# The last 64 keys of a block-causal attention: high and low halves of the probabilities on 128 partitions

## The chip, the core and the metric

The kernel runs on one core of a Trainium2 chip. The metric is the device time of one execution in microseconds (us). PE is TensorE, with its weight loads as a row of their own (PEld); DVE is VectorE, ACT is ScalarE, POOL is GpSimd and SP is SyncE, which issues most DMA transfers here.

## The reference

Attention over 4 batches, 8 heads, 576 positions and head dimension 64, whose output goes through two expert layers. Positions are in nine blocks of 64; a query sees the keys of its own block and of all blocks before it.

```python
scores = scale * np.matmul(q, k.transpose(0, 1, 3, 2))
mask = block_i >= block_j                  # block = position // 64
attn = softmax(np.where(mask, scores, -1e9))
x = np.matmul(attn, v)                     # (4, 8, 576, 64) -> rows of 512
x = moe(x, ...)                            # top 2 of 8 experts, 512 -> 1024 -> 512
out = moe2(x, ...)                         # one of 8 experts, with a bias by modality
```

The change is in the attention alone.

## The kernel before, in words

Attention goes through 16 pairs of heads (`pair(p)`, line 849). Numbers are split into a high part, rounded to the type that TensorE takes in one pass, and a low part, the rest; a product is hi x hi + hi x lo + lo x hi or, for the values, two halves side by side.

For each pair:

- `TQ`, `TK` and `T4` transpose q and k on PE, 128 positions at a time; `T4` (line 896) does the last 64 positions of q and of k, each as a transpose of 64 partitions. ACT writes the high parts (`qh` with its blocks in tiles named `kp`, `kh`), DVE the low ones (`ql`, `kl`).
- `S0` to `S8` are the scores of the nine query blocks, both heads on the 128 partitions of one product: three matmuls each (`ps<-kh,kp`, `ps<-kl,kp`, `ps<-kh,kp`). `M` is the row maximum on DVE (`nm`), `E` the exponential on ACT, which writes the strips `p` and sums the rows into `ss`. `R` adds the two sums of the last block, `R1` adds 1e-9 to the nine sums (`ss`, 128x9), `R2` makes their reciprocals (four `RECIPROCAL rr<-ss`).
- `B0` to `B5` transpose the probabilities, 128 keys by 128 columns at a time (`pt<-ident,p`), up to four in one PSUM bank; ACT copies the high part into `PTh` (`H`), DVE the low part into `PTl` (`L`). Of query block 8 the last 64 keys are left over: `BT` (line 1015) transposes them to 64 partitions, `HT` and `LT` write them to slot 28 of `PTh` and `PTl`. Slots 25 to 27 are zero on those partitions.
- `VX` and `V0`, `V1` (`av(h)`, line 1036) multiply by the values, `pa<-PTh,vs` and `pa<-PTl,vs`. The high and the low 64 columns of v are the 128 columns of the weights, so a full sum comes out as two halves of 64 partitions that `X0`, `X1` add (`pt<-IW,oT`). `V0` and `V1` have five matmuls for `PTh` and five for `PTl`: 448, 448, 320 and 256 columns with 128 keys each, and 256 columns with the last 64 keys on 64 partitions.
- `CX`, `C0`, `C1` and `XC0`, `XC1` are ACT's copies from PSUM (`oT`, `xu`). POOL multiplies the result by the reciprocals (`x` and the small `LH`, line 1067). It also splits v into high and low parts, `VS` (line 860): a cast and a subtraction for 128 partitions, and both again for the last 64 keys on 64.

Loads go through SP's queue (`load`, line 830): q and k three pairs ahead, v two. Of each tensor's tile of 128x5x2x64 the fifth chunk holds the last 64 positions on 64 partitions.

What stands where on PE, ACT and DVE is set by a planner (lines 1201 to 1350): a table of due times and costs for each kind of instruction, from which it places one step after the other on the engine that is free first. Three PSUM buffers serve all transposes and `X` products (`ps_t`), in turn: a new one waits until the last reader of the third one before it is done. Into the same engines it puts the routing of the experts after pairs 7, 11 and 15, a serial chain that is mostly DVE's (`sl_ob`, `sl_oa` are its one-hot tables, `sl_ov` POOL's product of them). After attention the expert layers follow, laid out by the same clock of planned costs.

Of the kernel before, what the change touches and what calls it, by code (L numbers as in the profile page):

```python
# [7 lines left out]
F32 = mybir.dt.float32  # L8
F32R = mybir.dt.float32r
BF16 = mybir.dt.bfloat16  # L10
I32 = mybir.dt.int32
AF = mybir.ActivationFunctionType
# [18 lines left out]
def moe_kernel(tc, q, k, v, w_gate, w_noise, noise, w1, w2, mod_id, w_gate2, mod_bias, m2w1, m2w2, out):  # L31
    nc = tc.nc
    B, H, S, D = q.shape
# [67 lines left out]
    gps = Timed(nc.gpsimd, "pool", pool_cost)  # L101
    vec, ten, act = Timed(nc.vector, "dve", dve_cost), Timed(nc.tensor, "pe", pe_cost), Timed(nc.scalar, "act", act_cost)

    with ExitStack() as top:
# [12 lines left out]
        ident = cst.tile([128, 128], F32, name="ident")  # L117
# [667 lines left out]
        with ExitStack() as ph:  # L785
            ld = ph.enter_context(tc.tile_pool(name="ld", bufs=3))
            aw = ph.enter_context(tc.tile_pool(name="aw", bufs=1))
# [3 lines left out]
            ps_t = ph.enter_context(tc.tile_pool(name="ps_t", bufs=bk[1], space=PSUM))  # L791
            ps_a = ph.enter_context(tc.tile_pool(name="ps_a", bufs=bk[2], space=PSUM))

            PTh = aw.tile([128, 29, 2, 64], F32R, name="PTh")
            PTl = aw.tile([128, 29, 2, 64], F32R, name="PTl")
            QB = [[keep.tile([128, 1280], F32R, name="kp%d" % (i + 2 * j))[:, 0:NB * 128].rearrange("p (b h s) -> p b h s", b=NB, h=2)
                   for j in range(2)] for i in range(2)]
            PW = [128 * ((i + 2) // 2) for i in range(8)] + [576]
# [28 lines left out]
            def copy(o, i):  # L827
                act.activation(o, i, AF.Copy)

            def load(p, names):  # L830
                b, hp = divmod(p, HP)
                r = L.setdefault(p, {})
                src = {"q": q, "k": k, "v": v}

                def ends():
                    for n in names:
                        nc.sync.dma_start(r[n][0:64, 4, :, :], src[n][b, 2 * hp:2 * hp + 2, 512:576, :].rearrange("h p d -> p h d"))
                for n in names:
                    r[n] = ld.tile([128, 5, 2, D], F32, name=n + "ld", bufs=2 if n == "v" else 3)
                if p:  # L840
                    ends()
                for n in names:
                    for i in range(2):
                        nc.sync.dma_start(r[n][:, 0:4, i, :],
                                          src[n][b, 2 * hp + i, 0:512, :].rearrange("(c p) d -> p c d", p=128))
                if not p:
                    ends()

            def pair(p):

                b, hp = divmod(p, HP)
                r = L[p]
                st = {}
                P = PP[p % 2]
                qh, ql = QB[0][p % 2], QB[1][p % 2]
                rr, xu = RR[p % 3], XU[p % 2]
                f = {}


                def VS():  # L860
                    vs = st["v"] = aw.tile([128, 5, 2, 2, D], F32R, name="vs", bufs=2)
                    for pp, c0, c1 in ((128, 0, 4), (64, 4, 5)):
                        hi = vs[0:pp, c0:c1, :, 0, :]
                        src = r["v"][0:pp, c0:c1]
                        gps.tensor_copy(hi, src)
                        gps.tensor_sub(vs[0:pp, c0:c1, :, 1, :], src, hi.bitcast(F32))

                def tr(n):
                    pt = ps_t.tile([128, 4, 128], F32, name="pt")
# [25 lines left out]

                def T4():
                    pt = ps_t.tile([128, 2, 64], F32, name="pt")
                    for i, n in enumerate("qk"):
                        ten.transpose(pt[:, i, :], r[n][0:64, 4].rearrange("p h d -> p (h d)"), ident[0:64, 0:64])
                    st["t4"] = pt  # L900

                def A4():
# [110 lines left out]
                    bank(m)  # L1013

                def BT():
                    st["bt"] = ps_t.tile([64, 128], F32, name="pt")
                    ten.transpose(st["bt"], P[8][:, 512:576], ident)

                end = lambda T: T[0:64, 28].rearrange("p h s -> p (h s)")
                f.update(BT=BT, HT=lambda: act.activation(end(PTh), st["bt"], AF.Copy),  # L1020
                         LT=lambda: vec.tensor_sub(end(PTl), st["bt"], end(PTh).bitcast(F32)))


                w = lambda j, h, n=128: st["v"][0:n, j, h].rearrange("p a d -> p (a d)")

                def VX():
                    pX = st["ax"] = ps_a.tile([128, 2, 256], F32, name="pa")
# [8 lines left out]
                def av(h):  # L1036
                    def V_():
                        pa = st["a", h] = ps_a.tile([128, 448], F32, name="pa")
                        for i, T in enumerate((PTh, PTl)):
                            ten.matmul(pa, w(0, h), T[:, 2:9, h, :], start=(i == 0), stop=False)  # L1040
                            ten.matmul(pa, w(1, h), T[:, 9:16, h, :], start=False, stop=False)
                            ten.matmul(pa[:, 128:448], w(2, h), T[:, 16:21, h, :], start=False, stop=False)
                            ten.matmul(pa[:, 192:448], w(3, h), T[:, 21:25, h, :], start=False, stop=False)
                            ten.matmul(pa[:, 192:448], w(4, h, 64), T[0:64, 25:29, h, :], start=False, stop=(i == 1))
                    f["V%d" % h] = V_
                    f["C%d" % h] = lambda: copy(st["oT"][:, h, 128:576], st["a", h])

# [44 lines left out]
            pads(0)  # L1092
            nc.gpsimd.memset(PTh[:, 21].bitcast(F32), 0.0)
            nc.gpsimd.memset(PTl[:, 21].bitcast(F32), 0.0)
            nc.gpsimd.memset(PTh[0:64, 25:28].bitcast(F32), 0.0)
            nc.gpsimd.memset(PTl[0:64, 25:28].bitcast(F32), 0.0)
            zeros(1, gps)
            pads(1)

# [206 lines left out]
            while any(todo.values()) or len(aside) > 1 or "early" not in flags:  # L1306
                best = None
                for e, l in todo.items():
                    c = []
                    for i, (due, p, n) in enumerate(l[:60]):  # L1310
                        t = earliest(e, p, n)
                        if t is not None:
                            c.append((t, due, i))
                    if c:
                        m = min(c)[0]
                        t, _, i = min((x for x in c if x[0] <= m + eps), key=lambda x: x[1])
# [6 lines left out]
                if aside:  # L1323
                    t = max(aside[0][0], clk["dve"])
                    if best is None or t <= best[0] and (t <= dve_next or t > aside[0][0] + patience):
                        best = (t, None, 0)
                t, e, i = best
# [3 lines left out]
                if e:  # L1331
                    _, p, n = todo[e].pop(i)
# [6 lines left out]
                else:  # L1339
                    clk["base"] = t  # L1340
                    d = next(aside[0][1], None)
# [204 lines left out]
        with tc.For_i(0, nc.values_load(more[0:1, 0:1], min_val=0, max_val=1), 1), tc.tile_pool(name="r1", bufs=1) as r1:  # L1546
# [12 lines left out]
            with tc.For_i(0, nc.values_load(eo[0:1, NG2:], min_val=0, max_val=NG2), 1):  # L1559
                NT2 = G2 // 128  # L1560
                a, bl = done(row_col(r1, ovs.rearrange("p c k -> p (c k)"), 2 * nb))
                pl = ps_r.tile([128, NV, NT2], F32, name="pt")
                for i in range(B):
                    n = slice(10 * i, 10 * i + 10)
# [12 lines left out]
                for t in range(NT2):  # L1577
                    xr = rp.tile([128, DM], F32, name="xr", bufs=5)
                    gps.indirect_dma_start(out=xr, out_offset=None, in_=X1, in_offset=bass.IndirectOffsetOnAxis(ap=ido[:, t:t + 1], axis=0))
                    pt = ps_x.tile([128, 4, 128], F32, name="px")  # L1580
# [4 lines left out]
                h = [hs[f][0].bitcast(F32) for f in range(NF // 128)]  # L1585
                for f in range(NF // 128):
                    w = r1.tile([128, 4, 128], F32, name="ow", bufs=2)
# [6 lines left out]
                for f in range(NF // 128):  # L1594
                    w = r1.tile([128, DM], F32, name="ow", bufs=2)
# [20 lines left out]
            with tc.For_i(0, nc.values_load(er[0:1, NG2:], min_val=0, max_val=NG2), 1):  # L1616
                prev_out.clear()
                ic = lambda t: idr[:, t:t + 1]
                j = group(m2w1, m2w2, X2, lambda: nc.sync.value_load(er[0:1, 0:1], min_val=0, max_val=E - 1), ic,
                          lambda t: gtr[:, t:t + 1], put_rows(ic))  # L1620
                st = Stage([j])
# [39 lines left out]
```

## Time and profile before

| what | us |
|---|---|
| median of 3 runs | 1046.46 (1046.31 to 1047.7) |
| profiled execution | 1041.64 |
| its span, first to last instruction | 1039.6 |
| PE busy | 987.5 (95%) |
| DVE busy | 741.4 (71%) |
| POOL busy | 534.2 (51%) |
| ACT busy | 518.9 (50%) |

The mean granted clock of TensorE is 0.983 of full speed. Attention takes some 300 us of the span, the expert layers the rest. The time of one matmul in the rows is longer than the distance to the next one's start, since matmuls are pipelined; a row with a count (x4) merges instructions that follow each other, under the name of the first, and lasts until the last one's end.

### The profile page before, as it was taken

How to read it: one execution, taken by the hardware profiler on the slowest of the kernel's cores; microseconds unless marked ns; L12 is line 12 of the kernel's file. 1: busy time of each engine (PE TensorE's matmuls, PEld its weight loads, DVE VectorE, ACT ScalarE, POOL GpSimd, SP SyncE). 2: the span in 40 equal slices, each digit the busy share in tenths (PEclk: the TensorE clock that was granted, in tenths of full speed). 3: DMA queues.
4: the chain of work that ended last, by engine and by line, in shares of the span. 5: the costliest groups of instructions: out<-in, count | busy, mean ns of one | idle time of the engine just before them, and what ended most of it. 6: DMA issues, size and time to landing. Idle time of an engine off the chain costs nothing.

```text
span 1039.6 us, 17514 instructions
## 1 busy us (share of the span) xinstructions
PE 987.5 (95%) x6090; PEld 879.0 (85%) x6090; DVE 741.4 (71%) x1766; ACT 518.9 (50%) x1156; POOL 534.2 (51%) x420
## 2 busy tenths in 40 slices
PE   7999998997998799999999999999999999999996
PEld 6888887776787789898989899898978888999995
DVE  6778779888868689647768493948798885554551
ACT  5887876766654225333333333333324545555651
POOL 6123142272346558977668584847658345333231
PEclk8999998998999899999999999999999999999999
DMA  5465433321117455655545372735167767677630
GB/s 127 110 189 163 147 97 96 89 60 39 54 55 212 163 122 132 182 144 134 111 125 120 104 142 81 158 87 102 16 179 204 259 187 253 217 224 225 205 103 13
DMA packets 155954, 141.08 MB, mean 136 GB/s; under 512 B 73929, under 2 KB 122441, under 8 KB 155730
## 3 DMA queue, kind: packets, MB, share of 16 engines
q1 hardware_dynamic: 137794, 106.65, 34.2%
q0 software_dynamic: 18064, 33.23, 15.8%
q8 instruction: 51, 0.84, 0.3%
q14 instruction: 45, 0.37, 0.1%
HBM read 112.01 MB, written 28.36 MB: 135 GB/s over the span
## 4 chain that ended last, share of the span: by engine, by line
PE 49%; issue 4%; POOL 3%; DVE 2%; DMA 1%; ACT 0%; POOLq 0%; SPq 0%
PE ph L71 25%; PE py L71 22%; PE px L71 2%; POOL wl L71 2%; DMA xr<-X,ids 1%; DVE wl L71 1%; POOL LG L71 0%; DMA raw<-in_moe_w_dram 0%; POOL X L71 0%; DMA lgx<-LG 0%; PE pt L71 0%; DVE g_l L71 0%; POOL out_dram L71 0%; DVE g_t L71 0%; DVE kp L71 0%
## 5 line engine op out<-in xcount | busy, mean ns | idle before, releaser
L71 POOL TENSOR_TENSOR wl<-raw,wh 128x1024 fp32r<-128x1024 f32 x88 | 226.8, 2618 | 120.0 <-ACT wh L71 108.1
L71 PE MATMUL ph<-xth,wh 128*128 128x320 f32 (+2 forms) x800 | 242.1, 303 | 6.5 <-DVE kp L71 6.5
L71 PE MATMUL ph<-xtl,wh 128*128 128x320 f32 (+2 forms) x800 | 240.7, 301 | 0.0
L71 PE MATMUL ph<-xth,wl 128*128 128x320 f32 (+2 forms) x800 | 240.6, 301 | 0.0
L71 DVE SCALAR_TENSOR_TENSOR zero<-py,gts,wgb 128x512 f32<-128x512 f32 x304 | 227.5, 748 | 8.2
L71 PE MATMUL py<-wh,kp 128*128 128x512 f32 x496 | 167.9, 399 | 0.0
L71 PEld LDWEIGHTS ph<-xth,wh 128*128 128x128 f32 x800 | 152.4, 190 | 8.2 <-DVE kp L71 7.5
L71 PEld LDWEIGHTS ph<-xtl,wh 128*128 128x128 f32 x800 | 152.5, 191 | 0.7
L71 PEld LDWEIGHTS ph<-xth,wl 128*128 128x128 f32 x800 | 152.4, 190 | 0.0
L71 ACT ACTIVATE wh<-raw 128x1024 fp32r<-128x1024 f32 x144 | 150.9, 1053 | 0.6 <-DMA raw<-in_moe_w_dram 0.4
L71 ACT ACTIVATE yr<-py,gts 128x512 f32<-128x512 f32 x60 | 41.4, 690 | 147.7 <-PE py L71 104.9
L71 PEld LDWEIGHTS py<-wh,kp 128*128 128x128 f32 x496 | 93.9, 189 | 18.7
L71 DVE SCALAR_TENSOR_TENSOR hl<-ph,hh 128x320 fp32r<-128x320 f32 (+2 forms) x100 | 46.4, 466 | 76.3 <-ACT hh L71 76.3
L71 PE MATMUL ps<-kh,kp 128*128 128x256 f32 (+5 forms) x320 | 98.4, 349 | 2.2 <-ACT kp L71 1.0
L71 PE MATMUL py<-wl,kp 128*128 128x512 f32 x248 | 97.2, 392 | 0.0
L71 PE MATMUL py<-wh,hh 128*128 128x512 f32 x232 | 93.9, 405 | 0.0
L71 DVE TENSOR_TENSOR xtl<-px,xth 128x512 fp32r<-128x512 f32 x58 | 40.0, 690 | 74.3 <-ACT xth L71 68.2
L71 PE MATMUL py<-wl,hh 128*128 128x512 f32 x232 | 90.6, 390 | 1.3 <-POOL wl L71 1.3
L71 PE MATMUL py<-wh,hl 128*128 128x512 f32 x232 | 90.8, 391 | 0.0
L71 ACT ACTIVATE p<-ps,nm 128x288 f32<-128x288 f32 (+8 forms) x160 | 79.1, 500 | 22.4 <-DVE nm L71 20.8
L71 DVE TENSOR_TENSOR wl<-raw,wh 128x1024 fp32r<-128x1024 f32 x56 | 70.0, 1259 | 27.8 <-ACT wh L71 27.4
L71 ACT ACTIVATE hh<-ph 128x320 fp32r<-128x320 f32 (+2 forms) x100 | 41.9, 419 | 94.4 <-PE ph L71 91.2
(250 smaller groups left out, 1886.5 us busy)
## 6 DMA issues: line engine op xcount, KB each, us to landing
raw<-in_moe_w_dram SPq DMA_DIRECT2D x144, 512.0 KB
X<-zero SPq DMA_DIRECT2D x13, 512.0 KB
kld<-in_k_dram SPq DMA_DIRECT2D x32, 128.0 KB
qld<-in_q_dram SPq DMA_DIRECT2D x32, 128.0 KB
vld<-in_v_dram SPq DMA_DIRECT2D x32, 128.0 KB
X<-x SPq DMA_DIRECT2D x16, 256.0 KB
xs<-in_moe_w_dram SPq DMA_DIRECT2D x4, 512.0 KB
wgb<-WG2T POOLq DMA_DIRECT2D x1, 2048.0 KB
```

The lines of the kernel that those rows point to most:

```text
L71: return f(*a, **kw)
```

## The change

- The probabilities of the last 64 keys. `BT` now makes two transposes into one tile of 128 partitions: a full one of columns 448 to 575, whose lower 64 partitions are the last 64 keys, and one of columns 512 to 575 over the upper 64 partitions. Both halves then hold the same keys. `HT` writes the high part on all 128 partitions of slot 28 of `PTh`; `LT` replaces the second half by the low part. `PTl` ends at slot 24.
- The values. The last 64 keys of v are loaded twice, to partitions 0 to 63 and 64 to 127 of the fifth chunk, and `VS` splits 128 partitions in one cast and one subtraction.
- `V0` and `V1` then need one matmul with 128 rows for the last keys where there were two with 64: nine matmuls each, all with full weights.
- The last 64 positions of q and of k come into one tile `tld`, q on the first 64 partitions and k on the others, and `T4` is one transpose of 128 partitions.

```diff
-            PTl = aw.tile([128, 29, 2, 64], F32R, name="PTl")
+            PTl = aw.tile([128, 25, 2, 64], F32R, name="PTl")
...
+                if names == "v":
+                    r["v"] = ld.tile([128, 5, 2, D], F32, name="vld", bufs=2)
+                    tails = [(r["v"][64 * i:64 * i + 64, 4], "v") for i in range(2)]
+                else:
+                    r["t"] = ld.tile([128, 2, D], F32, name="tld")
+                    tails = [(r["t"][64 * i:64 * i + 64], n) for i, n in enumerate("qk")]
...
                 def ends():
-                    for n in names:
-                        nc.sync.dma_start(r[n][0:64, 4, :, :], src[n][b, 2 * hp:2 * hp + 2, 512:576, :].rearrange("h p d -> p h d"))
+                    for t, n in tails:
+                        nc.sync.dma_start(t, src[n][b, 2 * hp:2 * hp + 2, 512:576, :].rearrange("h p d -> p h d"))
...
-                    for pp, c0, c1 in ((128, 0, 4), (64, 4, 5)):
-                        hi = vs[0:pp, c0:c1, :, 0, :]
-                        src = r["v"][0:pp, c0:c1]
-                        gps.tensor_copy(hi, src)
-                        gps.tensor_sub(vs[0:pp, c0:c1, :, 1, :], src, hi.bitcast(F32))
+                    hi = vs[:, :, :, 0, :]
+                    gps.tensor_copy(hi, r["v"])
+                    gps.tensor_sub(vs[:, :, :, 1, :], r["v"], hi.bitcast(F32))
...
-                    for i, n in enumerate("qk"):
-                        ten.transpose(pt[:, i, :], r[n][0:64, 4].rearrange("p h d -> p (h d)"), ident[0:64, 0:64])
+                    ten.transpose(pt.rearrange("p i s -> p (i s)"), r["t"].rearrange("p h d -> p (h d)"), ident)
...
-                    st["bt"] = ps_t.tile([64, 128], F32, name="pt")
-                    ten.transpose(st["bt"], P[8][:, 512:576], ident)
+                    st["bt"] = ps_t.tile([128, 128], F32, name="pt")
+                    ten.transpose(st["bt"], P[8][:, 448:576], ident)
+                    ten.transpose(st["bt"][0:64], P[8][:, 512:576], ident)
...
-                end = lambda T: T[0:64, 28].rearrange("p h s -> p (h s)")
-                f.update(BT=BT, HT=lambda: act.activation(end(PTh), st["bt"], AF.Copy),
-                         LT=lambda: vec.tensor_sub(end(PTl), st["bt"], end(PTh).bitcast(F32)))
+                end = PTh[:, 28].rearrange("p h s -> p (h s)")
+                f.update(BT=BT, HT=lambda: act.activation(end, st["bt"], AF.Copy),
+                         LT=lambda: vec.tensor_sub(end[64:128], st["bt"][64:128], end[64:128].bitcast(F32)))
...
-                            ten.matmul(pa[:, 192:448], w(3, h), T[:, 21:25, h, :], start=False, stop=False)
-                            ten.matmul(pa[:, 192:448], w(4, h, 64), T[0:64, 25:29, h, :], start=False, stop=(i == 1))
+                            ten.matmul(pa[:, 192:448], w(3, h), T[:, 21:25, h, :], start=False, stop=(i == 1))
+                            if i == 0:
+                                ten.matmul(pa[:, 192:448], w(4, h), PTh[:, 25:29, h, :], start=False, stop=False)
```

Since the planner sees other costs, some steps stand in another order. On PE the undisturbed pairs keep theirs; the second head's value products and what follows them, before:

```order
L71 MATMUL pa<-PTh,vs 128x448 x2
L71 MATMUL pa<-PTh,vs 128x320
L71 MATMUL pa<-PTh,vs 128x256 x2
L71 MATMUL pa<-PTl,vs 128x448 x2
L71 MATMUL pa<-PTl,vs 128x320
L71 MATMUL pa<-PTl,vs 128x256 x2
L71 MATMUL pt<-ident,p_174 64x128
L71 MATMUL pt<-ident,p_166 128x128
```

The same place on PE with the change:

```order
L71 MATMUL pa<-PTh,vs 128x448 x2
L71 MATMUL pa<-PTh,vs 128x320
L71 MATMUL pa<-PTh,vs 128x256 x2
L71 MATMUL pa<-PTl,vs 128x448 x2
L71 MATMUL pa<-PTl,vs 128x320
L71 MATMUL pa<-PTl,vs 128x256
L71 MATMUL pt<-ident,p_174 128x128
L71 MATMUL pt<-ident,p_174 64x128
L71 MATMUL pt<-ident,p_166 128x128
```

One matmul is gone and one transpose stands ahead of `BT`'s 64-column one; nothing else moved there.

On DVE, at the end of each undisturbed pair's scores, before (`ss` 128x1 is `R`, `PTl` 64x128 is `LT`, `ss` 128x9 is `R1`; the next `PTl` 128x512 are `L0` and `L3`):

```order
L71 TENSOR_TENSOR ss<-ss 128x1
L71 TENSOR_TENSOR PTl<-pt,PTh 64x128
L71 TENSOR_SCALAR ss<-ss 128x9
L71 TENSOR_REDUCE nm<-ps 128x1
L71 TENSOR_TENSOR PTl<-pt,PTh 128x512 x2
```

The same place on DVE with the change (`PTh` 64x128 is now `LT`):

```order
L71 TENSOR_TENSOR ss<-ss 128x1
L71 TENSOR_SCALAR ss<-ss 128x9
L71 RECIPROCAL rr_161<-ss 64x5
L71 RECIPROCAL rr_161<-ss 64x4
L71 RECIPROCAL rr_161<-ss 64x5
L71 RECIPROCAL rr_161<-ss 64x4
L71 TENSOR_TENSOR PTh<-pt,PTh 64x128
L71 TENSOR_REDUCE nm<-ps 128x1
L71 TENSOR_TENSOR PTl<-pt,PTh 128x512 x2
```

`R1` and the four reciprocals moved ahead of `LT`; the reciprocals stood seven rows further down, behind the last bank's `PTl`.

## Rows read from the trace of the kernel before

**Rows 1.** Windows: us, busy us (instructions) by engine, clock, DMA share, GB/s.

```profile
20.00:40.00 20.00, 19.80 (x124) 17.57 (x125) 15.94 (x40) 15.19 (x47) 2.53 (x4) 0.91 0.54 101
...
220.00:240.00 20.00, 14.08 (x92) 11.69 (x91) 16.43 (x26) 10.44 (x33) 10.90 (x9) 0.89 0.26 71
...
280.00:300.00 20.00, 19.30 (x132) 16.10 (x131) 15.27 (x53) 11.18 (x35) 6.48 (x6) 1.00 0.11 30
```

**Rows 2.** The page's chain that ended last, shares of the span by engine.

```profile
PE 49%; issue 4%; POOL 3%; DVE 2%; DMA 1%; ACT 0%; POOLq 0%; SPq 0%
```

**Rows 3.** Timeline, POOL: start us, us, operation, count [idle before <- releaser].

```profile
98.81 1.26 POOL L71 TENSOR_TENSOR x<-xu,rr 128x640 f32<-128x640 f32 x1 [12.55 <-DVE kp L71]
100.23 0.84 POOL L71 CAST vs<-vld 128x512 fp32r<-128x512 f32 x2 [0.16 <-PE pa L71]
101.04 1.72 POOL L71 TENSOR_TENSOR vs<-vld,vs 128x512 fp32r<-128x512 f32 x2
...
114.82 1.26 POOL L71 TENSOR_TENSOR x<-xu,rr 128x640 f32<-128x640 f32 x1 [11.65 <-DVE kp L71]
```

**Rows 4.** Timeline, PE, one pair: matmuls with full weights.

```profile
102.19 0.36 PE L71 MATMUL ps<-kl,kp 128*128 128x448 f32 x1
102.39 0.37 PE L71 MATMUL ps<-kh,kp 128*128 128x448 f32 x1
102.60 0.60 PE L71 MATMUL pt<-ident,p 128*128 128x128 f32 x4
...
104.71 0.60 PE L71 MATMUL pt<-ident,p 128*128 128x128 f32 x4
105.06 0.36 PE L71 MATMUL pa<-PTh,vs 128*128 128x256 f32 x1
105.27 0.28 PE L71 MATMUL pa<-PTl,vs 128*128 128x256 f32 x1
105.38 0.28 PE L71 MATMUL pa<-PTh,vs 128*128 128x256 f32 x1
```

**Rows 5.** Timeline, PE, the same pair: first head's value products, then T4.

```profile
108.01 1.24 PE L71 MATMUL pa<-PTh,vs 128*128 128x448 f32 x5
...
110.27 0.21 PE L71 MATMUL pt<-ident,qld 64*128 64x64 f32 x1
...
110.72 0.29 PE L71 MATMUL ps<-kl,kp 128*128 128x288 f32 x1
```

**Rows 6.** Timeline, PE: second head's value products, then BT and four transposes.

```profile
113.74 1.25 PE L71 MATMUL pa<-PTh,vs 128*128 128x448 f32 x5
...
116.10 0.74 PE L71 MATMUL pt<-ident,p 128*64 128x128 f32 x5
```

**Rows 7.** Timeline, ACT, the same pair.

```profile
110.59 0.45 ACT L71 ACTIVATE kp<-pt 64x64 fp32r<-64x64 f32 x2 [0.84 <-PE pt L71]
...
112.01 1.20 ACT L71 ACTIVATE kp<-pt 64x512 fp32r<-64x512 f32 x2 [0.30 <-PE pt L71]
```

**Rows 8.** Timeline, DVE, the same pair.

```profile
98.83 1.25 DVE L71 TENSOR_TENSOR ss<-ss 128x1 f32<-128x1 f32 x1
100.73 0.28 DVE L71 TENSOR_TENSOR PTl<-pt,PTh 64x128 fp32r<-64x128 f32 x1 [0.65 <-ACT PTh L71]
...
101.72 1.41 DVE L71 TENSOR_TENSOR PTl<-pt,PTh 128x512 fp32r<-128x512 f32 x2
...
106.97 0.75 DVE L71 RECIPROCAL rr<-ss 64x5 f32<-64x5 f32 x4
```

**Rows 9.** Timeline, DVE: two places where the scaling of `ss` (R1) lasts long.

```profile
84.03 1.42 DVE L71 TENSOR_SCALAR ss<-ss 128x9 f32<-128x9 f32 x1
...
231.67 4.96 DVE L71 TENSOR_SCALAR ss<-ss 128x9 f32<-128x9 f32 x1
```

**Rows 10.** Timeline, PE: its first wait after each of the two.

```profile
86.58 0.63 PE L71 MATMUL pt<-ident,p 128*128 128x128 f32 x4 [0.73 <-DVE PTl L71]
...
238.46 1.12 PE L71 MATMUL pt<-ident,p 128*128 128x128 f32 x4 [5.47 <-DVE PTl L71]
```

More of the change, by code (lines that the diff above doesn't have):

```diff
@@ L833, in load @@
                 src = {"q": q, "k": k, "v": v}
+                if names == "v":
[4 more added lines that the diff above has]
+                    tails = [(r["t"][64 * i:64 * i + 64], n) for i, n in enumerate("qk")]
+                    for n in names:
+                        r[n] = ld.tile([128, 4, 2, D], F32, name=n + "ld")
                 def ends():
-                    for n in names:
-                        nc.sync.dma_start(r[n][0:64, 4, :, :], src[n][b, 2 * hp:2 * hp + 2, 512:576, :].rearrange("h p d -> p h d"))
-                for n in names:
-                    r[n] = ld.tile([128, 5, 2, D], F32, name=n + "ld", bufs=2 if n == "v" else 3)
+                    for t, n in tails:
+                        nc.sync.dma_start(t, src[n][b, 2 * hp:2 * hp + 2, 512:576, :].rearrange("h p d -> p h d"))
                 if p:
@@ L1015, in BT @@
                 def BT():
-                    st["bt"] = ps_t.tile([64, 128], F32, name="pt")
-                    ten.transpose(st["bt"], P[8][:, 512:576], ident)
-                end = lambda T: T[0:64, 28].rearrange("p h s -> p (h s)")
-                f.update(BT=BT, HT=lambda: act.activation(end(PTh), st["bt"], AF.Copy),
-                         LT=lambda: vec.tensor_sub(end(PTl), st["bt"], end(PTh).bitcast(F32)))
-                w = lambda j, h, n=128: st["v"][0:n, j, h].rearrange("p a d -> p (a d)")
+                    st["bt"] = ps_t.tile([128, 128], F32, name="pt")
[4 more added lines that the diff above has]
+                         LT=lambda: vec.tensor_sub(end[64:128], st["bt"][64:128], end[64:128].bitcast(F32)))
+                w = lambda j, h: st["v"][:, j, h].rearrange("p a d -> p (a d)")
                 def VX():
@@ L1094, in moe_kernel @@
             nc.gpsimd.memset(PTl[:, 21].bitcast(F32), 0.0)
-            nc.gpsimd.memset(PTh[0:64, 25:28].bitcast(F32), 0.0)
-            nc.gpsimd.memset(PTl[0:64, 25:28].bitcast(F32), 0.0)
+            nc.gpsimd.memset(PTh[:, 25:28].bitcast(F32), 0.0)
             zeros(1, gps)
```

## The prediction

> **What bounds the kernel now.** I read the table of windows first. From 20 to 300 us the kernel is in attention, and in ten of the fourteen 20-us windows there PE is busy for 19 us or more; in the other four it is less, 14.1 us in the lowest, while DVE works on the expert routing [rows 1]. So most of attention is limited by what PE issues, and the four others by a serial DVE chain. After attention the chain that ended last is nearly all PE again [rows 2], so time taken from attention should reach the end of the run.
>
> A busy PE hides a lot, because a matmul lasts longer than the distance to the next one's start. What counts is that distance, which I call pitch. I read it from PE's timeline in the pair of heads between 98 and 118 us. Two pairs are 16.0 us apart there: POOL's product `x` starts at 98.81 and at 114.82 [rows 3].
>
> **Prices.** With full 128x128 weights a matmul of 256 columns starts 0.11 us before the next (105.27 to 105.38), one of 448 columns 0.20 us (102.19 to 102.39), so 320 columns take about 0.14 us, one third of the way up. Four transposes take 0.35 us (104.71 to 105.06), of which the last gives way after some 0.03; the matmul behind them pays 0.21 instead of 0.11 us [rows 4].
>
> **PE, step by step.**
> - *The value products.* Each head has ten matmuls, two of them on 64 partitions. The first head's block lasts 108.01 to 110.27, 2.26 us [rows 5]; the second's 113.74 to 116.10, 2.36 us [rows 6]. By the prices, nine full matmuls take 0.30 (448 columns behind a change) + 3 x 0.20 + 2 x 0.14 + 3 x 0.115 = 1.53 us. So the change takes 0.73 + 0.83 = 1.56 us from a pair. It is far more than the 0.11 us of each matmul that goes: of the first block's 2.26 us the eight full matmuls take 1.53 - 0.11 = 1.42, and 0.84 are left for two 64-row ones. Each costs 0.42 us, its own 0.11 and some 0.3 for changing the rows in use, going in and coming out. A neighbouring price for the new matmul speaks the same: it looks like any full one.
> - *The ends of q and k.* Two 64-row transposes and the matmul behind them take 110.27 to 110.72, 0.45 us [rows 5]. One full transpose gives way after 0.03 and the matmul behind it takes about 0.22: 0.25 us. Gain 0.20 us.
> - *The end of the probabilities (BT).* The 64-column transpose stays, at 116.10 behind the second block [rows 6], and a full one now stands ahead of it. It adds at least its own 0.11 us (0.35 less the last one's 0.03, by three), and at most 0.31 with a change of 0.2 more (the two changes of a 64-row matmul cost 0.3 together). I take 0.20, as only the way in is new.
> - Sum: 1.56 + 0.20 - 0.20 = **1.56 us** less PE per pair, with bounds of 1.4 and 1.7. The period would fall from 16.0 to 14.4 us if nothing else were late.
>
> The Trainium skill (TensorE: Matmul & The Clock Gate, Part 3, The mechanism) says that a weight load overlaps with running matmuls only where the row group differs. By that rule the 64-row loads would be the hidden ones and only 0.11 us of columns would go with each matmul; the 0.42 us of the trace speaks against it. I keep it as a rival below.
>
> **What is late next.** ACT and DVE now wait for PE in each block: ACT idles 0.84 us before `kp` at 110.59 and 0.30 before the one at 112.01 [rows 7]. Those 1.14 us are what that leg can shrink: the softmax of the next strips, the copy to `xu` and the POOL product `x` behind it come at most 1.1 us earlier per pair. From there on the leg is DVE's, and the order of the change makes it tighter. Now DVE does `ss` (which lasts 1.25 us at 98.83 for one element per partition, exactly while POOL's `x` runs 1.26 us), waits for the transposed end, subtracts it (`PTl` at 100.73), and comes to the first bank at 101.72; the four reciprocals follow only at 106.97 [rows 8]. `x` is in [rows 3]. After the change the scaling of `ss` and the four reciprocals (0.75 us) stand ahead of that subtraction. They fit in the wait that is there now (98.83 + 1.25 = 100.08 to 100.73, 0.65 us) and in the time that the scaling no longer takes later. So the leg from `x` to the first bank's `PTl` stays as long as it is, 101.72 - 98.81 = 2.9 us, while PE wants to come some 0.5 us earlier. PE's transposes at 102.60 [rows 4] need the PSUM buffer that this `PTl` frees about 0.7 us after 101.72. PE will wait there about half a microsecond.
>
> The trace shows that this leg has little to give: at 84.03 the scaling lasted 1.42 us, and PE waited 0.73 us before its transposes at 86.58 [rows 9, 10]. So of 1.56 us per pair I count the **1.05 us** that ACT's waits allow, between 0.75 (if the reciprocals are not wholly hidden) and 1.56 (PE's sum, nothing late).
>
> **Other engines.** On POOL the split of v goes from four instructions to two over the same columns and 128 partitions: now 0.84 us of casts from 100.23 and 1.72 of subtractions [rows 3]; no longer after, and nothing waits for it but the next pair's value products, 8 us on. SP issues one more 32 KB transfer per pair and the ends of q and k go to one tile. The loads are issued two and three pairs ahead, 32 us or more, so the cost is nothing unless that lead is lost; PE would then show waits on DMA, and none is among its waits in these pairs. I leave it inside the 3 us below. ACT's copy and DVE's subtraction of the end keep their 128 columns.
>
> **The sum.** Ten windows of 20 us are 200 / 16.0 = 12.5 pairs: 12.5 x 1.05 = 13.1 us. In the other four windows, some four pairs, DVE sets the pace; I count 1.5 us in all (0 to 4). One event there should go. At 231.67 the scaling of `ss` lasted 4.96 us behind POOL's work on the routing tables, and PE stood for 5.47 us until 238.46 [rows 9, 10]. In the new order the scaling comes ahead of the two one-hot operations that start that POOL work. I count 2 us (0 to 5). Together 16.6 us, say 16.5. Of the profiled execution, 1041.64 us, 1025.1 would be left. The runs' median is 1046.46, 4.8 us above the profiled one; the gain is one of work, so I take it from the median: **1030.0 us**. The later stages are planned anew from another clock, which I give 3 us either way.
>
> **Rivals.**
> 1. *PE's sum comes through whole*: DVE and ACT keep up. 12.5 x 1.56 = 19.5, + 4 + 3 = 26 us: 1020. For it: ACT and DVE are busy 15.2 and 15.9 of 20 us, some 12 to 13 of a 16-us pair [rows 1]. Against it: the wait at 86.58.
> 2. *The scaling of ss falls behind POOL's cast.* It now follows `ss` at once, so about when `x` ends and the cast of v starts, 0.16 us later (98.81 + 1.26 = 100.07; 100.23) [rows 3]. If the cast comes first, its 0.84 us delay every `PTl` of the pair: 1.05 - 0.84 = 0.2 us per pair, 2.6 + 3.5 = 6 us: 1040.
> 3. *Slower: the scaling waits for all of POOL's split of v* (0.84 + 1.72 = 2.56 us, and the small `LH` that now stands between them), as it waited 4.96 us at 231.67 behind several operations. The pair then takes 16.0 - 1.05 + 2.56 = 17.5 us, 1.5 x 12.5 = 19 us more: 1065. It decides from a delay of 1.05 us per pair on. Against it: a small operation that already waited when `x` ended got in at once (`ss` ended with `x`), and the cast needs 0.16 us to start. The Trainium skill (SBUF — State Buffer, SBUF: two separate sides) says that whichever of VectorE and GpSimd starts first holds their shared port for the whole instruction; the 1.25 beside the 1.26 us agrees, and rivals 2 and 3 are that rule at another place.
> 4. *Only columns count.* A 64-row matmul would cost what its 256 columns cost: 32 x 0.11 = 3.5 us, less 16 x 0.11 for the added transpose = 1.8 us: 1044.7. That is also what the rule on row groups above would give. The trace's 0.42 us is against it.
>
> **How the numbers follow.** A measurement of this kernel can tell about 0.2%, 2 us, from no change. My forecast has 0.52 (1024 to 1036), rival 1 0.14, rival 2 0.17, rival 4 0.05, rival 3 0.07, and 0.05 for a reordered routing stretch that eats or doubles the gain, of either sign. Rivals 1 and 2 reach to 1018 and 1044, so 1021 to 1041 holds the forecast, most of rival 2 and half of rival 1, about 0.8. Faster by over 0.2%: 0.52 + 0.14 + 0.16 + 0.04 = 0.86. Same: 0.06. Slower: 0.08.
>
> **What the profile after would show.** Value blocks of about 1.5 us instead of 2.3, the weights of the last keys loaded ahead like the others. `x` starting some 15 us apart in the undisturbed pairs; 14.4 would be rival 1, 15.8 rival 2, over 16 rival 3. A new wait of PE before its transposes, released by DVE's `PTl`, of half a microsecond, once per pair. The scaling of `ss` lasting 0.2 us and not 0.9 or more. PE idle before 238 us gone or shorter. A value block that still lasts 2 us would make the whole forecast wrong; waits of PE on DMA would make the part on SP wrong.

## The result

The changed kernel takes 1021.66 us (median of four runs, 1020.32 to 1022.09), the kernel before 1046.38 us on the same chip: a ratio of 0.976, 95% interval 0.9745 to 0.9779, or 24.7 us less. Beside the experiments, on another chip, it was 0.980 (0.976 to 0.984). The prediction was 1030.0 us with a range of 1021 to 1041: the time lies in the range, just above its lower end, and the gain of 16.5 us was put 8 us too low.

### The profile after

The changed kernel's windows (us; busy us and instructions of PE, PEld, DVE, ACT, POOL; clock, DMA share, GB/s), beside [rows 1], and the last stretch of 20 us that has a large hole:

```profile
20.00:40.00 20.00, 17.57 (x115) 16.15 (x115) 17.25 (x44) 14.94 (x46) 2.27 (x2) 0.91 0.50 92
...
220.00:240.00 20.00, 17.93 (x131) 15.83 (x130) 18.55 (x44) 15.20 (x46) 10.82 (x7) 1.00 0.26 73
280.00:300.00 20.00, 20.00 (x147) 18.48 (x146) 13.52 (x46) 10.87 (x25) 10.67 (x12) 1.00 0.52 167
300.00:320.00 20.00, 11.63 (x68) 10.28 (x66) 18.83 (x23) 7.47 (x11) 17.32 (x8) 0.89 0.83 215
```

The window from 220 to 240 us held 14.08 us of PE before and holds 17.93 now (the same time, but not the same work: the changed kernel's pairs are 7 to 16 us ahead there). Between 300 and 320 us stands a hole that is longer than the one which the kernel before has at its place; a section below is on it.

PE's timeline, one undisturbed pair of the changed kernel (start us, us, operation, count [idle before <- releaser]), beside [rows 5, 6]:

```profile
91.23 1.04 PE L71 MATMUL pa<-PTh,vs 128*128 128x448 f32 x5
92.11 0.84 PE L71 MATMUL pa<-PTl,vs 128*128 128x448 f32 x4
92.79 0.27 PE L71 MATMUL pt<-ident,tld 128*128 128x128 f32 x1
92.81 0.38 PE L71 MATMUL ps<-kh,kp 128*128 128x288 f32 x1
93.03 0.30 PE L71 MATMUL ps<-kl,kp 128*128 128x288 f32 x1
...
96.06 1.05 PE L71 MATMUL pa<-PTh,vs 128*128 128x448 f32 x5
96.95 0.83 PE L71 MATMUL pa<-PTl,vs 128*128 128x448 f32 x4
97.62 0.82 PE L71 MATMUL pt<-ident,p 128*128 128x128 f32 x6
98.19 0.40 PE L71 MATMUL ps<-kh,kp 128*128 128x320 f32 x1
...
100.18 0.66 PE L71 MATMUL pt<-ident,p 128*128 128x128 f32 x4 [0.86 <-DVE PTh L71]
```

PE's own work fell as forecast. The value blocks last 91.23 to 92.79 and 96.06 to 97.62, 1.56 us each (2.26 and 2.36 before). T4 and the matmul behind it last 92.79 to 93.03, 0.24 us (0.45). But PE now waits 0.86 us before the transposes at 100.18. Here is what it waits for, on POOL and DVE in the same pair, beside [rows 3, 8]:

```profile
97.14 1.26 POOL L71 TENSOR_TENSOR x<-xu,rr 128x640 f32<-128x640 f32 x1 [11.88 <-ACT xu L71]
98.34 0.72 POOL L71 CAST vs<-vld 128x640 fp32r<-128x640 f32 x1
99.02 0.46 POOL L71 TENSOR_TENSOR LH<-xu,rr 128x160 f32<-128x160 f32 x1
99.43 1.56 POOL L71 TENSOR_TENSOR vs<-vld,vs 128x640 fp32r<-128x640 f32 x1
112.87 1.26 POOL L71 TENSOR_TENSOR x<-xu,rr 128x640 f32<-128x640 f32 x1 [11.88 <-DMA qld<-in_q_dram]
```

```profile
97.36 1.05 DVE L71 TENSOR_TENSOR ss<-ss 128x1 f32<-128x1 f32 x1
98.52 0.57 DVE L71 TENSOR_SCALAR ss<-ss 128x9 f32<-128x9 f32 x1
99.19 0.75 DVE L71 RECIPROCAL rr<-ss 64x5 f32<-64x5 f32 x4
99.86 0.27 DVE L71 TENSOR_TENSOR PTh<-pt,PTh 64x128 fp32r<-64x128 f32 x1
...
100.68 1.29 DVE L71 TENSOR_TENSOR PTl<-pt,PTh 128x512 fp32r<-128x512 f32 x2
```

ACT, whose waits before its `kp` were 0.84 and 0.30 us [rows 7], has none left there:

```profile
93.09 0.45 ACT L71 ACTIVATE kp<-pt 64x64 fp32r<-64x64 f32 x2
...
94.33 1.19 ACT L71 ACTIVATE kp<-pt 64x512 fp32r<-64x512 f32 x2
```

`x` is 112.87 - 97.14 = 15.73 us apart, against 16.0 before: of 1.6 us of PE work that went, 0.27 us arrive. The sum of `ss` (R) ends with `x`, the scaling (R1, 128x9) with the cast of v, the reciprocals follow, and only then comes LT (`PTh` 64x128), for which PE waits. That is rival 2 of the prediction, and yet the run came out near rival 1's 1020 us. So most of the gain is elsewhere. The table cuts the profiled executions at five places of PE's timeline (the first head's value block of the 9th and of the 13th pair, the last `pt<-IW,oT`, the first `ph` of the expert layers, the end of the span). The last three columns are experiments that follow.

| stretch, us | before | changed | new work, old order | old work, new order | sums late |
|---|---|---|---|---|---|
| to the 9th pair | 159.9 | 156.9 (-3.0) | -11.1 | -0.9 | -12.2 |
| 9th to 13th pair, most of the routing | 84.5 | 71.7 (-12.8) | -6.1 | -8.2 | -8.9 |
| to the last product of attention | 60.3 | 52.9 (-7.4) | -5.4 | -2.1 | -5.0 |
| to the first expert product | 27.9 | 23.6 (-4.2) | 0.0 | -4.2 | -6.1 |
| to the end | 707.0 | 713.4 (+6.4) | +0.7 | +7.5 | +0.7 |
| span | 1039.6 | 1018.5 (-21.0) | -21.9 | -7.9 | -31.5 |

The first value block starts at 28.8, 29.1, 28.8, 27.7 and 29.2 us in these five executions, and at 25.9 in another execution of the changed kernel; of a difference in the first line that part says nothing of the change.

### The profile page after: what moved, and what is told of

Read it like the earlier page. It is cut to its first block, busy times and chain, and to the rows that moved or that the text cites. A ratio compares the mean times of both kernels' runs of the same rounds, so it can differ in the third digit from the quotient of the medians.

```text
span 1018.5 us, 17480 instructions
## 1 busy us (share of the span) xinstructions
PE 960.6 (94%) x6058; PEld 867.4 (85%) x6058; DVE 733.8 (72%) x1766; ACT 519.0 (51%) x1156; POOL 528.5 (52%) x387
## 4 chain that ended last, share of the span: by engine, by line
PE 74%; DVE 13%; issue 4%; ACT 3%; POOL 2%; DMA 2%; SPq 1%; POOLq 0%; DVEq 0%; ACTq 0%
PE ph L71 29%; PE py L71 25%; PE pt L71 8%; PE ps L71 6%; PE pa L71 4%; PE px L71 2%; POOL wl L71 1%; DVE ss L71 1%; DVE kp L71 1%; DVE zero L71 1%; DVE nm L71 1%; DVE PTl L71 1%; DMA wgb<-WG2T 1%; DMA xr<-X,ids 1%; DVE wl L71 1%
## 5 line engine op out<-in xcount | busy, mean ns | idle before, releaser
L71 POOL DMA_INDIRECT xr<-X,ids x55 | 58.1, 1057 | 62.2 <-PE px L71 47.4
```

Source lines behind the costliest of these rows:

```text
L71: return f(*a, **kw)
```

## The experiments

"Pairs" below is the distance of undisturbed pairs on PE, from one value block to that of the next pair. Each ratio is to the kernel before in runs on the same chip, whose median there was 1042.2 to 1044.4 us.

### Work and order apart

The change does two things: PE gets less to do, and the planner, which sees other costs, puts steps in another order. Two kernels cross the two, by correcting the planner's clock alone. New work in the old order is the changed kernel with these edits in BT, VS and V0, V1; old work in the new order is the kernel before with the opposite corrections of `clk` at the same three places. In both, all instructions of DVE and of ACT stand in the order that is meant:

```diff
-                    ten.transpose(st["bt"], P[8][:, 448:576], ident)
+                    nc.tensor.transpose(st["bt"], P[8][:, 448:576], ident)
...
+                    clk["pool"] += .12
...
+                        clk["pe"] += 256 * .000417
```

> The changed instructions, but the planner is told the costs of before, so that DVE and ACT run in the order of before, row for row, and PE differs only in the changed instructions. Work theory (the gain of 24.7 us is the time that PE no longer spends): about 1022, as the changed kernel, 15.7 us between pairs. Order theory (most of the gain comes from the new order around the routing stretches, where the scaling of ss no longer waits behind POOL's table product): 1033 to 1042; the scaling still lasts about 5 us near 230 us and PE stands 3 us or more behind it, while the undisturbed pairs, whose scaling stays behind LT, come 15.0 us apart or closer to 16.0.

Measured: 1023.3 us, ratio 0.982 (0.9795 to 0.9851), pairs 14.55 us.

> The instructions of before, but the planner is told the costs of the change, so that DVE and ACT run in the order of the changed kernel, row for row, and PE differs only in the changed instructions. Work theory: 1045 to 1050, no gain, and up to 0.3 us more per undisturbed pair (the scaling behind the cast). Order theory: 1026 to 1036; no scaling over 2 us in the routing stretches, the stretch from 160 to 244 us 9 to 12 us shorter, undisturbed pairs 16.0 to 16.8 us apart.

Measured: 1033.74 us, ratio 0.992 (0.989 to 0.994), pairs 16.1 us.

Neither theory has it alone. The work in the old order brings 1.8%, nearly the whole result, and it does so everywhere in attention: 1.45 us in each undisturbed pair, 6.1 / 4 = 1.5 us per pair in the routing stretch too. The new order with the old work brings 0.8%, of which 8.2 us in the routing stretch. Together they do not add, because the order that costs 0.1 us per undisturbed pair at PE's old pace costs 15.73 - 14.55 = 1.2 us per undisturbed pair at the new one. The rows show why. POOL and DVE in a pair of the old work in the new order:

```profile
113.71 1.26 POOL L71 TENSOR_TENSOR x<-xu,rr 128x640 f32<-128x640 f32 x1 [11.74 <-DMA kld<-in_k_dram]
115.13 0.84 POOL L71 CAST vs<-vld 128x512 fp32r<-128x512 f32 x2 [0.16 <-PE pa L71]
```

```profile
115.09 0.17 DVE L71 TENSOR_SCALAR ss<-ss 128x9 f32<-128x9 f32 x1
```

With the slower PE the cast waits 0.16 us for the value products (`<-PE pa`), and the scaling gets in between: 0.17 us. With the faster PE the cast is ready when `x` ends, the gap is gone, and the scaling lasts 0.57 us. The reciprocals stand ahead of LT in both; the slower PE left time for them, the faster one does not. What each of the two costs is measured further down.

In the routing stretch it is the other way round. DVE, POOL and PE in the new work in the old order:

```profile
216.27 3.20 DVE L71 TENSOR_SCALAR ss<-ss 128x9 f32<-128x9 f32 x1
```

```profile
215.91 3.53 POOL L71 TENSOR_TENSOR sl_ov<-sl_oa,vals 128x2000 bf16<-128x2000 bf16 x1
```

```profile
221.31 1.12 PE L71 MATMUL pt<-ident,p 128*128 128x128 f32 x4 [3.71 <-DVE PTl L71]
```

In the old order the scaling falls beside POOL's table product and ends with it, 219.4; PE stands 3.71 us. In the changed kernel it comes before the one-hot tables:

```profile
216.59 0.17 DVE L71 TENSOR_SCALAR ss<-ss 128x9 f32<-128x9 f32 x1 [0.62 <-ACT p L71]
...
218.79 2.44 DVE L71 TENSOR_TENSOR sl_ob<-lane,sl_b 128x1280 bf16<-128x1280 f32 x1 [1.17 <-PE pt L71]
```

In the kernel before it was caught even longer, at 231.67 [rows 9], by three of POOL's operations in a row:

```profile
231.43 0.46 POOL L71 TENSOR_TENSOR LH<-xu,rr 128x160 f32<-128x160 f32 x1
231.85 1.26 POOL L71 TENSOR_TENSOR x<-xu,rr 128x640 f32<-128x640 f32 x1
233.06 3.53 POOL L71 TENSOR_TENSOR sl_ov<-sl_oa,vals 128x2000 bf16<-128x2000 bf16 x1
```

It ended at 236.63, they at 236.59. The interval from the 12th to the 13th pair is 27.7 us before and 26.4 in the new work in the old order, but 18.6 in the changed kernel and 20.7 in the old work in the new order.

### The parts of the work

> The kernel before with one part of the change alone: the shared transpose T4 for the ends of q and k (and their loads into one tile); all engines keep the order of before. By the prediction's price of 0.20 us for a change of the rows in use, T4 and what follows take 0.25 instead of 0.45 us, undisturbed pairs come 15.8 us apart and the run is 3 us shorter. If only columns count, 16.0 us and no difference.

Measured: 1044.21 us, ratio 1.002 (0.9998 to 1.0048), pairs 15.95 us. It takes from the diff only the parts on `tld` and `T4`.

> The other part alone: last keys stacked on 128 partitions, nine matmuls per head, BT with its second transpose, T4 as before, and the planner told the costs of before, so that DVE and ACT keep the order of before. By the prediction's prices 0.73 + 0.83 - 0.20 = 1.36 us per pair: 14.6 to 14.7 us between undisturbed pairs, 15 to 17 us shorter, and with the shared transpose alone it sums to the 18.9 us of the new work in the old order. If fewer matmuls is all there is, 0.2 us per pair less one transpose: 15.9 us, 1 to 2 us shorter.

Measured: 1023.75 us, ratio 0.981 (0.977 to 0.985), pairs 14.9 us. It is the rest of the diff, with the planner told the costs of before.

> The changed kernel itself, beside the parts on one chip. Its ratio to the kernel before was 0.976, so 24 to 26 us shorter, 15.7 us between undisturbed pairs. If the parts sum (18.9 us for the new work in the old order, 8.5 us for the new order with the old work) it would be 27.4 us; what is less is what the new order costs the undisturbed pairs once PE is faster.

Measured: 1021.27 us, ratio 0.980 (0.976 to 0.984), pairs 15.7 us.

The parts do not sum: 0.05 us and 1.1 us per pair alone, 1.45 together. PE's timeline with the ends alone:

```profile
109.29 1.25 PE L71 MATMUL pa<-PTl,vs 128*128 128x448 f32 x5
110.47 0.33 PE L71 MATMUL pt<-ident,tld 128*128 128x128 f32 x1
110.56 0.38 PE L71 MATMUL ps<-kh,kp 128*128 128x288 f32 x1
```

The value block before it began at 108.13 and now lasts 2.34 instead of 2.26 us, and T4 with the matmul behind it 110.47 to 110.77, 0.30 us. In the kernel before, the block ends with a 64-row matmul and T4 has 64 rows too: one change of rows out of 64 serves both. Make T4 full, and that change is paid at the end of the value block. So the price is one of each change, not of each instruction. Beside the new value products the shared T4 is worth more, 14.89 - 14.55 = 0.34 us per pair: with the values alone the first head's block and T4 with the matmul behind it take 1.64 and 0.50 us, in the new work in the old order 1.55 and 0.24.

> The kernel before with its ten matmuls per head, but the two of the last keys on all 128 partitions: the probabilities on the upper 64 are zeros that stay, the last keys of v are loaded twice; BT and T4 as before, order of before. It has no matmul less. If a 64-row matmul pays some 0.3 us for changing the rows in use, a value block takes 9 x its present prices + 0.115 = 1.65 us instead of 2.3, pairs come 14.7 to 14.8 us apart and the run is 13 to 16 us shorter. If the gain is that of the matmul that goes, the block stays at 2.2 to 2.3 us, 16.0 us, no difference.

```diff
-                            ten.matmul(pa[:, 192:448], w(4, h, 64), T[0:64, 25:29, h, :], start=False, stop=(i == 1))
+                            ten.matmul(pa[:, 192:448], w(4, h), T[:, 25:29, h, :], start=False, stop=(i == 1))
...
-            nc.gpsimd.memset(PTh[0:64, 25:28].bitcast(F32), 0.0)
-            nc.gpsimd.memset(PTl[0:64, 25:28].bitcast(F32), 0.0)
+            nc.gpsimd.memset(PTh[:, 25:29].bitcast(F32), 0.0)
+            nc.gpsimd.memset(PTl[:, 25:29].bitcast(F32), 0.0)
```

Measured: 1018.11 us, ratio 0.977 (0.973 to 0.981), pairs 14.9 us. PE's timeline there:

```profile
103.00 1.04 PE L71 MATMUL pa<-PTh,vs 128*128 128x448 f32 x5
103.88 0.95 PE L71 MATMUL pa<-PTl,vs 128*128 128x448 f32 x5
104.76 0.27 PE L71 MATMUL pt<-ident,qld 64*128 64x64 f32 x1
```

Ten matmuls, none fewer than before, half of their rows zeros in the last two: 1.76 us instead of 2.26 (1.67 instead of 2.36 for the second head). Its pairs are as close as with the values alone. So the gain is that of not changing the rows in use; the matmul that the stacking saves is worth 0.11 us a head, and half of that goes to BT's added transpose. Over all it is as fast as the change, 24 us shorter where I expected 13 to 16, but that is not the rows alone: from the 12th to the 13th pair it takes 22.1 us, the values alone 28.5 with the same order. With the values alone the scaling met POOL's table product (3.20 us at 222.69); with the full rows it ended with `x`, ahead of that product (1.04 us at 219.21). The Trainium skill (TensorE: Matmul & The Clock Gate, Part 3, The mechanism) has weight loads overlap only where the row group differs, and has them pulled ahead where row groups do not conflict; the 64 rows are part of the 128, so rival 4 was wrong to take the 64-row loads for the hidden ones by it. Here the matmuls that come to another set of rows are the dear ones.

### Which step holds the undisturbed pairs

Three kernels keep the change and move steps of `ss` on DVE, by one more dependency in the planner's list (`L1` is the second bank's low part). With the sums late, R waits for it, and the scaling and the reciprocals come behind R:

```diff
-                      "R": E_, "BT": ["E8"], "HT": ["BT"], "LT": ["HT"], "VX": ["L0", "VS"], "CX": ["VX"], "V0": L_ + ["VS"], "V1": L_ + ["VS"],
+                      "R": E_ + ["L1"], "BT": ["E8"], "HT": ["BT"], "LT": ["HT"], "VX": ["L0", "VS"], "CX": ["VX"], "V0": L_ + ["VS"], "V1": L_ + ["VS"],
```

> The changed kernel with the sum R, the scaling R1 and the reciprocals of ss made after the second bank's low parts (L1), when POOL is idle. If the wait of PE in each undisturbed pair (0.86 us before the transposes of the first bank) comes from R and R1 standing behind POOL's product x and its cast (rival 2 of the prediction), R and R1 take 0.2 us each, the wait goes and pairs come 14.4 to 15.0 us apart: 1010 to 1018, unless the routing stretches lose what they gained, as these operations may again meet POOL's table product. If PE is held by something else, 15.6 to 15.8 us and 1020 to 1024.

Measured: 1011.16 us, ratio 0.970 (0.968 to 0.973), pairs 14.5 us.

With the scaling late R stays, and the scaling waits, with the reciprocals behind it:

```diff
-"R1": ["R"]
+"R1": ["R", "LT"]
```

> The changed kernel with only the scaling R1 and the reciprocals made to wait for LT; the planner then puts them after all banks, and R stays under POOL's x. If the scaling behind the cast is what costs (0.57 us and then the four reciprocals of 0.75 us ahead of LT), pairs come 14.6 to 15.2 us apart: 1012 to 1018 with the routing stretches as they are. If R alone, blocked until x ends, is what costs, 15.5 to 15.7: 1019 to 1022.

Measured: 1022.26 us, ratio 0.980 (0.978 to 0.983), pairs 14.5 us.

With the reciprocals late the scaling stays too:

```diff
-"R2": ["R1"]
+"R2": ["R1", "L1"]
```

> The changed kernel with only the four reciprocals made later (after the second bank's low parts); the scaling R1 stays where the change puts it, ahead of LT and behind POOL's cast. With the scaling and the reciprocals both late, pairs come 14.5 us apart, in the changed kernel 15.7. If the scaling behind the cast is the cost (rival 2 as the prediction had it), 15.4 to 15.7. If the 0.75 us of reciprocals between it and LT are the larger part, 14.8 to 15.0. If the two add on one chain, 15.73 - 0.75 = 15.0. The routing stretches keep the new order, so the run is 1009 to 1016 where before is 1042.

Measured: 1016.1 us, ratio 0.9745 (0.972 to 0.977), pairs 15.0 us.

The chain adds up: 0.73 us (15.73 to 15.00) are the reciprocals ahead of LT, 0.5 us (15.00 to 14.5) the scaling behind the cast, and R under `x` costs nothing there. DVE with the reciprocals late, and then with the sums late:

```profile
94.18 1.05 DVE L71 TENSOR_TENSOR ss<-ss 128x1 f32<-128x1 f32 x1
95.34 0.57 DVE L71 TENSOR_SCALAR ss<-ss 128x9 f32<-128x9 f32 x1
95.94 0.29 DVE L71 TENSOR_TENSOR PTh<-pt,PTh 64x128 fp32r<-64x128 f32 x1
```

```profile
98.86 0.15 DVE L71 TENSOR_TENSOR ss<-ss 128x1 f32<-128x1 f32 x1
99.04 0.17 DVE L71 TENSOR_SCALAR ss<-ss 128x9 f32<-128x9 f32 x1
```

Away from POOL the two take 0.15 and 0.17 us instead of 1.05 and 0.57. With sums late, no scaling in the whole of attention lasts over 0.2 us. With the scaling and the reciprocals late but R under `x`, the undisturbed pairs are as close, but in the routing stretch the scaling stands behind the one-hot tables again (3.2 us at 216.3), the interval to the 13th pair is 26.7 us, and the gain of the pairs is lost: my expectation of 1012 to 1018 had forgotten that the same wait stands there.

> The kernel before with nothing of the change, but with the sum R, the scaling R1 and the reciprocals made after the second bank's low parts, as in the kernel with late sums. If the order alone brings what the routing stretches gain, no scaling of ss lasts over 1 us there and the run is 7 to 14 us shorter than before (the new order with the old work gave 8.5 us); the undisturbed pairs, which PE's own work limits at 16.0 us, come 15.9 to 16.0 us apart. If late sums also help undisturbed pairs without the change, 15.0 to 15.7 us apart and 15 to 22 us shorter. If late sums need the time that the change frees, no gain at all.

Measured: 1025.54 us, ratio 0.984 (0.980 to 0.988), pairs 16.0 us: the kernel before with the late sums alone. That is 18.8 us less, more than the 7 to 14 that I expected. In its undisturbed pairs PE is the limit and nothing moves. Of the 16.9 us that its profiled execution is shorter, 5.0 lie between the 9th and the 13th pair, 2.8 from there to the last product of attention and 6.1 from that to the first expert product; 3.4 lie ahead of the first value block, which moves by nearly as much between two executions of the changed kernel, 0.9 in the one pair that the scaling at 84.03 had made longer, and 1.3 go in the expert layers. The late sums alone are worth as much as the change's work in the old order, and the two nearly add (1.6% and 1.8%, together 3.0%).

### The hole at 311 us, and the best version

In the changed kernel the last stretch gives 6.4 us back, as it does in the old work in the new order (7.5). DVE and POOL of the changed kernel, and PE:

```profile
309.41 8.29 DVE L71 COPY base<-pos 128x8 f32<-128x8 f32 x1
...
319.31 0.55 DVE L71 SCALAR_TENSOR_TENSOR kp<-ph,kp 128x384 fp32r<-128x384 f32 x1
```

```profile
310.14 7.52 POOL L71 TENSOR_TENSOR wl<-raw,wh 128x1024 fp32r<-128x1024 f32 x3
```

```profile
319.91 0.69 PE L71 MATMUL ph<-xth,wh 128*128 128x384 f32 x1 [8.37 <-DVE kp L71]
```

A copy of eight numbers per partition lasts 8.29 us and ends with three weight splits of POOL, and PE stands 8.37 us for the subtraction queued behind it on DVE. In the old work in the new order it is the same copy (8.29 us), and PE stands 8.32. In the kernels with another order another small operation is caught at this place (8.02 us in the new work in the old order, 7.74 with sums late), and PE stands about 5 us. The kernel before has a hole there too, behind 7.89 us of a `TENSOR_SCALAR` on five elements:

```profile
342.94 0.69 PE L71 MATMUL ph<-xth,wh 128*128 128x384 f32 x1 [3.96 <-DVE kp L71]
```

So the hole is 4.4 us longer now. Ahead of the first expert product it is the other way round: before, PE waited 3.79 us at 326.8 for a step of the routing (`m`), and now does not. So the two stretches belong together, and over both 2.2 us are lost. Behind the expert product that starts at 387.1 us before and at 366.1 now, the two kernels keep a distance of 21.0 to 21.2 us to the end.

I tried to shorten POOL's run, on top of the sums late:

```diff
-                run([j00, j10, j11] + firsts, hidden(hp1), [gps], [gps], seconds[0])
+                run([j00, j10, j11] + firsts, hidden(hp1), [gps], [vec, gps], seconds[0])
```

> The kernel with late sums (R after L1), and of the splits of the next experts' weights in the first expert layer every second one on DVE instead of POOL. There three splits in a row kept POOL busy for 7.6 us from 304 us on, and a DVE operation on ten elements per partition lasted 7.7 us beside them (the same with 8.3 us on eight elements in the changed kernel), for which PE stood 5.4 us. If the blocked operation is the cause, it lasts 5 us or less, PE's wait shrinks by 2 to 4 us and the run is 2 to 5 us shorter than with late sums alone. If DVE is simply full there, the added 1.1 us per split makes it 0 to 4 us longer.

Measured: 1028.95 us, ratio 0.986 (0.983 to 0.989). Locally it did what the blocked operation asks for (5.42 instead of 7.73 us, beside two splits instead of three), and PE's wait for `kp` from 300 to 330 us fell from 5.3 to 3.6 us; a wait for a gather grew by 0.7 and one for `sl_ov` by 0.8 us. The later stages lost some 20 us, 15 of them between 730 and 830 us, where DVE now has more to do and POOL's transfers go out at other times; PE waits there 3.0 us for `sl_ov`, 3.8 for a gather and 4.7 for `g_oh`, and the granted clock was 0.87 from 740 to 780 us and 0.94 from there to 840, against 1.00 with the sums late. Which of these made the loss was not tried.

> The kernel with late sums once more, beside the two others: 0.970 of the kernel before, 1010 to 1012 us where before is 1042, and 14.5 us between undisturbed pairs.

Measured: 1009.52 us, ratio 0.9685 (0.966 to 0.971), pairs 14.5 us. With 0.970 in its other run this is the fastest version, about a percent faster than the change, for one more dependency in the planner's list.

## Why the prediction was right, and where it was not

- *The prices of PE* held. Value blocks of 1.56 us (1.53 forecast), T4 and the matmul behind it 0.24 (0.25), BT's added transpose 0.11: BT and the four transposes behind it take 0.57 us with the values alone (108.77 to 109.34) and 0.46 with the full rows, which lack it (109.97 to 110.43). That is the least price that I gave; I took 0.20. Against the kernel before it is 0.08 (97.62 to 98.19 is 0.57 us, before 0.49 behind a 64-row matmul). PE's sum is 0.80 + 0.70 + 0.21 - 0.08 = 1.6 us per pair. That a 64-row matmul pays for the rows and not for its columns was shown by the ten full matmuls; rival 4 is out. T4's 0.20 us belongs to it only beside the new value products; alone it brought 0.05.
- *The step that failed first* is the leg on DVE in undisturbed pairs. The prediction had the scaling and the reciprocals fit into the wait that stood ahead of LT, and counted 1.05 us per pair. Measured: 0.27. The reciprocals cost 0.73 us, the scaling 0.5. Rival 2, to which I gave 0.17, did happen, and its 0.2 us per pair is near the 0.27, but its scaling is the smaller part; the larger is the reciprocals, which I had bounded at 0.3 us. Against rival 3, whose scaling waits at the same place, I had argued that the cast needs 0.16 us to start after `x`. The row itself said otherwise: the idle time at 100.23 was ended by `PE pa` [rows 3]. The gap was PE's lateness, and it goes when PE gets faster. And what stood in a wait as long as PE was slow was no longer in a wait.
- *The step that failed second* is the term for the stretches where DVE routes: 1.5 us, with 2 us for the block at 231.67. From the 9th pair to the end of attention the profiled execution gained 20.2 us. Two halves of that were mis-sized. PE's freed time counts there in full (6.1 us over four pairs and 5.4 over the last ones with the work in the old order); that PE is not busy all the time did not mean that its time is free. And the block at 231.67 is worth more than my 2 us: with the order alone the interval from the 12th to the 13th pair shrinks from 27.7 to 20.7 us. That the scaling would leave POOL's table product behind was right.
- The two errors had opposite signs: some 10 us too much in the undisturbed pairs, some 17 us too little in the routing stretch and behind it. That the time still lies in the range, 0.7 us above its lower end, is luck. Of the 24.7 us the profiled executions show 21.3; the rest is that the profiled one before was 4.7 us under its median and the one after 1.3. The time came out near rival 1, whose reason, all of PE's sum in undisturbed pairs, did not hold in the changed kernel; it does hold with the old order (14.55 us) and with the sums late.
- *The later stages* moved by 4.2 us one way and 6.4 the other. Together they lose 2.2 us, inside the 3 us that I allowed, but only because the two nearly cancel.
- *Signs*: the new wait of PE once per pair was there, 0.86 us instead of half a microsecond, and put down to LT (`PTh`) rather than the first bank. The scaling of 0.57 us, not 0.2, and 15.7 instead of 15 us between pairs pointed to rival 2. The transfers on SP cost nothing: no undisturbed pair shows a wait of PE on DMA.
- *Left open*: how much of the 24.7 us is the new order's net share. The work in the old order gives 0.982 and the change 0.976 and 0.980, with intervals that overlap; the two profiled spans differ by 0.9 us.

## What to carry to other kernels

A matmul of 256 columns that uses 64 rows between full ones cost three to four times its columns here, so fill the array, with zeros if need be; where two short ones stand together, they share the price. When PE gets faster, look again at every operation that now hides in a wait for PE, and at what ended each gap: a gap released by the engine that you speed up will close. And keep small SBUF-to-SBUF operations of DVE out of POOL's busy stretches, above all where the next thing queued behind them on DVE is what PE waits for.

## What the runs showed of the hardware

- A DVE operation on a few elements can last as long as POOL's operations beside it, and through several that follow each other without a gap: R 0.15 us alone and 1.05 beside `x`, the scaling 0.17 alone and 4.96 beside `LH`, `x` and `sl_ov` [rows 9], a copy 8.29 beside three weight splits. The Trainium skill (SBUF — State Buffer, SBUF: two separate sides) has the one that starts first hold the shared port for a whole instruction; these rows agree. A gap of 0.16 us was enough for DVE to get in. Without a gap it goes both ways: at 98.52 the scaling ends with the cast although `LH` follows at once, at 231.67 it passes the ends of `LH` and of `x`. What decides that is not shown.
- Not all DVE operations wait: the reciprocals took 0.75 us for four beside POOL and 0.74 away from it, and LT, which reads PSUM, took 0.27 us in the middle of POOL's subtraction of v.
- The price of changing the rows in use is paid once per change (the value block took 0.08 us more when T4 became full), so two neighbouring 64-row instructions share it.
